# Four segments of attention and feed-forward on one core: the first segment's head in single tiles, and the issue order of all five engines written out as a table

## The chip, the cores and the metric

One core of one Trainium2 chip runs the whole program. The metric is device time in microseconds (us) of one execution, the median of three runs; each compared pair runs on the same chip. A profiled execution of each kernel gives its trace.

## What is computed

The input is 2048 tokens of 640 features in bfloat16. Two rounds of the same two blocks are applied, each added to its input:

```python
x = x + _A_ref(_layernorm(x), wq, wk, wv, wo, beta)   # attention with a memory
x = x + _B_ref(_layernorm(x), w1, w2)                 # relu(x @ w1) @ w2, 640 -> 1728 -> 640
x = x + _A_ref(_layernorm(x), wq, wk, wv, wo, beta)
x = x + _B_ref(_layernorm(x), w1, w2)
```

Block A has 32 heads of 20 features and works through 4 segments of 512 tokens. In each segment it takes causal softmax attention inside the segment, and reads a linear memory `M, z` that the earlier segments have written:

```python
logits = einsum('bhqd,bhkd->bhqk', qs, ks) * scale + mask
a_dot  = softmax(logits) @ vs
a_mem  = (phi(qs) @ M) / (phi(qs) @ z + 1e-6)
outs  += [g * a_mem + (1 - g) * a_dot]
M, z   = M + phi(ks)^T vs, z + sum(phi(ks))
```

## The kernel before

The tokens stand as 16 tiles of 128 (`x_sb`), four to a segment. For each segment the kernel normalizes four tiles (`lnorm`, or `first_pair` for the very first segment), turns them so that features lie on partitions (`xnT`), projects to queries, keys and values, and copies the results from the eight PSUM banks to SBUF. Queries and keys (`stg`) are written to a scratch tensor in DRAM (`spill`, tiles `scr`) and read back by head into `pad` (`fill`), where four heads of 20 rows each lie in four strips of 32 partitions. A fill is four DMAs, one for each strip.

TensorE (PE) then works on pairs of head groups: 8 score halves after each other (`scores`, tiles `ps<-pad`, line L1114), which ScalarE turns into probabilities (`exps`, L1166, tile `PT`) and GpSimd masks (`causal`, L1178); and the value pass (`apply`, L1257, `ps<-PT,v_aug`). Scores use the PE array in four strips of rows, value passes in four strips of columns, everything else uses the whole array. VectorE copies value results out (`av`, L1265), a DMA turns them (`avt`), and `divide` and `combine` make `o_sb`. Then follow the output projection, layer norm and feed-forward (L651 and L654 are the lines of all matmul groups, L1405 the last feature chunk). The memory is read at L1007 (`mem_read`) and written at L1058 (`mem_write`). Where the planner foresees that PE would wait, `keep_busy` puts matmuls of an identity matrix on it (L638, `ps<-ident`), whose results nobody reads; 43 of them warm it at the start (L634).

Everything is written as about 45 streams, generators that yield one operation at a time. The planner `Sched.run` holds a model of the time of each engine and, again and again, takes the operation that can start first, with a priority for each stream. Each engine gets a fixed list, with semaphore waits between engines, so an instruction that waits holds up everything behind it on its engine. SyncE (SP) issues nearly all DMAs, in its own fixed order. The planner runs with 48 values of one cost; `late` replays each plan with DMAs that land late at random, and the plan with the least time is built:

```python
STARTS = [SWITCH_NS + 0.75 * (k - 48 // 2) for k in range(48)]                 # L161
plans = [plan(k, sb, sem_, ...) for k in STARTS]
S = min(plans, key=lambda p: sum(p.late(n) for n in range(4)))
S.P.emit(block)
```

In the head, tiles 0 and 1 of the first segment are one stream (`first_ln_a`: both halves of the statistics at L662, the aggregate at L664, `lnU` at L672, the power on GpSimd at L676, then the normalization `xn_tok` at L716), tiles 2 and 3 another (`first_ln_b`: tile 2's mean and variance by two passes on ScalarE, L764 and L768, tile 3's statistics on VectorE). PE turns each tile with five small matmuls (L739), VectorE or ScalarE copies the result to `xnT` (L745, L746), and `proj_first` projects two tiles at a time, 256 columns wide.

Of the kernel before, what the change touches and what calls it, by code (L numbers as in the profile page):

```python
# [6 lines left out]
dt = mybir.dt  # L7
ACT = mybir.ActivationFunctionType
ALU = mybir.AluOpType
# [164 lines left out]
HOLD_TOL = {"pe": 220.0, "act": 150.0, "dve": 200.0, "pool": 0.0, "sp": 0.0}  # L174


class Sched:


    def __init__(self, prog, switch):  # L180
        self.P = prog
        self.switch = switch
        self.log = []
        self.free = {e: 800.0 for e in ENGS}
        self.t = {}
        self.events = {}
        self.streams = []
        self.dma_free = 0.0
        self.pe_mode = "full"
        self.spare = []  # L190
        self.idle_fn = None

    def keep_busy(self, op, start):

        gap = start - self.free["pe"]
        if gap < IDLE_NS or self.idle_fn is None:
            return
        own = self._pick(op.acq) if op.acq is not None else None
        s = self._pick([x for x in self.spare if x is not own])
        if s is None:  # L200
            return
        begin = max([self.free["pe"]] + [self.at(t) + SEM_NS for t in s.tks])
        n = int((start - begin - IDLE_NS / 2) // (56.0 if begin > COLD_NS else 107.0))
        if n > 1:
            self.log.append(("pe", 56.0 * n, 0.0, s.tks, [], False))
            self.P.waits("pe", s.tks)
            for _ in range(n):
                self.P.op("pe", lambda e, ap=s.ap: self.idle_fn(e, ap), False)

    def add(self, prio, gen):  # L210
        self.streams.append([prio, gen, None, None, False])
# [59 lines left out]
    def run(self):  # L271
        while True:
# [76 lines left out]
            else:  # L349
# [5 lines left out]
                        marks.append(tk)  # L355
                out = marks[0] if len(marks) == 1 else (marks or None)
            self.log.append((e, hold, tail, waits, out if isinstance(out, list) else [out], op.dma is not None))
            st[2], st[3] = None, ((slot, out) if slot is not None else out,)

    def late(self, seed):  # L360

# [26 lines left out]
def pe(ns, fns, waits=(), acq=None, take=(), mode="full"):  # L388
    return Op([("pe", ns, fns, 190.0)], waits, acq=acq, take=take, mode=mode)
# [29 lines left out]
def plan(switch, sb, sem_, psum, dram, A_x, A_wq, A_wk, A_wv, A_wo, A_beta, B_x, B_w1, B_w2, out):  # L419
# [248 lines left out]
    def chain(t0, n, tk, sq=None):  # L668

        sl = slice(t0, t0 + n)  # L670
        if sq is None:
            tk = yield dve(n, 1, lambda e: e.tensor_scalar(lnU[:, sl], mv[:, sl, 1], LN_EPS, None, ALU.add), tk)  # L672
# [3 lines left out]
        tk = yield pool(760, lambda e: e.tensor_tensor(rstd[:, sl], lnU[:, sl], mhalf[:, 0:n], ALU.pow), [tk] + h)  # L676
        return tk

    def turn(slot_sem, dst, src, waits, lat=2000.0):
# [35 lines left out]
    def normed(t, k, bx, tch):  # L715
        return dve(D, 4, lambda e: e.tensor_scalar(  # L716
            bx.ap[:, k * D:k * D + D], x_sb[:, t, :], mv[:, t, 0:1], rstd[:, t:t + 1],
            ALU.subtract, ALU.mult), [tch] + bx.tks, extra=120)

    def first_pair(p, tch):  # L720
        idt = yield Need("ident")
        if p == 0:
            xt = yield Acq(XNT_A)
            xt.users = []
            S.set("xts", 0, 0, tks=[xt])
        else:
            xt = yield Need("xts", 0, 0)
            xt = xt[0]
        bx = yield Acq(XN)
        done = []  # L730
        tns = []
        for k in range(2):
            tn = yield normed(2 * p + k, k, bx, tch[k])
            tns.append(tn)
        for k in range(2):
            t = 2 * p + k
            tn = tns[k]
            pb = lambda bk: bk.ap.bitcast(dt.bfloat16)
            fns = [(lambda e, bk, c=c, k=k: e.transpose(  # L739
                pb(bk)[:, c * 128:(c + 1) * 128], bx.ap[:, k * D + c * 128:k * D + c * 128 + 128], ident[:]),  # L740
                c == FC - 1) for c in range(FC)]
            bk, tT = yield pe((88.0 if p == 0 else 56.0) * FC, fns, [tn] + idt, acq=MISC)
            dst = xt.ap[:, t * FC:(t + 1) * FC, :].rearrange("p c n -> p (c n)")
            src = pb(bk)[:, 0:D]
            tc = yield evac(D, 1.5, lambda e, dst=dst, src=src: e.tensor_copy(dst, src),  # L745
                            lambda e, dst=dst, src=src: e.activation(dst, src, ACT.Copy), [tT])  # L746
            bk.release(tc)
            done.append(tc)
        bx.release(tT)
        S.set("xt", 0, 0, p, tks=done)  # L750

    def first_ln_a():
        tch = []
        for t in range(2):
            w = yield Need(("x0a", "x0b")[t])
            tk = yield from stats(t, w)
            tk = yield from chain(t, 1, [tk])
            tch.append(tk)
        yield from first_pair(0, tch)

    def first_ln_b():
        w = yield Need("x01")
        junk = hT[:, 10:13, :].rearrange("p c n -> p (c n)")[:, 0:D]
        t0 = yield act(D + 350, lambda e: e.activation(  # L764
            junk, x_sb[:, 2, :], ACT.Copy, accum_out=asum[:, 0:1]), w, psum=False)
        tm = yield dve(2, 1, lambda e: e.tensor_scalar(
            mv[:, 2, 0:1], asum[:, 0:1], 1.0 / D, None, ALU.mult), [t0])
        t1 = yield act(D + 470, lambda e: e.activation(  # L768
            junk, x_sb[:, 2, :], ACT.Square, scale=-1.0, bias=mv[:, 2, 0:1],
            accum_out=asum[:, 2:3]), [tm], psum=False)  # L770
        t3 = yield from stats(3, w)
        t1 = yield dve(1, 1, lambda e: e.tensor_scalar(
            lnU[:, 2:3], asum[:, 2:3], 1.0 / D, LN_EPS, ALU.mult, ALU.add), [t1])
        t3 = yield dve(1, 1, lambda e: e.tensor_scalar(lnU[:, 3:4], mv[:, 3, 1:2], LN_EPS, None, ALU.add), [t3])
        h = yield Need("mhalf")
        tch = yield pool(760, lambda e: e.tensor_tensor(
            rstd[:, 2:4], lnU[:, 2:4], mhalf[:, 0:2], ALU.pow), [t1, t3] + h)
        yield from first_pair(1, [tch, tch])


    def proj_ln(a, s):
# [27 lines left out]
    def proj_part(a, s, c, n, h):  # L809
# [767 lines left out]
```

## Time and profile before

| | |
|---|---|
| time, median of 3 runs | 562.49 us (562.12 to 563.04) |
| the profiled execution's own time | 562.46 us |
| its span in the trace | 560.6 us, so 1.86 us lie outside |
| instructions in the trace | 12651 |
| busy share: PE, VectorE (DVE), ScalarE (ACT), GpSimd (POOL) | 99%, 73%, 73%, 35% |

The page gives the busy time of each engine, the span in 40 slices, the DMA queues, the chain of work that ended last, and the costliest groups of instructions. In the timeline a row is: start in us, duration in us, engine, line, operation, output tile `<-` input tiles, shapes, and how many equal instructions it merges; a bracket tells the idle time before it and what ended it. A matmul's duration in a row includes its way through the array, so rows of PE overlap; the spacing between the starts of two rows tells how long the first one held the array.

### The profile page before, as it was taken

The numbers are of one execution on the slowest core, as the hardware profiler recorded it, in microseconds if no ns is written. First come the engines' busy times: TensorE is split into PE (matmuls) and PEld (weight loads), VectorE is DVE, ScalarE is ACT, GpSimd is POOL, SyncE is SP. The second block draws the span as 40 slices with busy tenths as digits, with TensorE's granted clock in tenths as the row PEclk, the third lists the DMA queues.
The fourth block names the chain that finished last, engine by engine and source line by source line (L and its number), as shares of the span: only waits on it lengthen the run. The fifth ranks groups of instructions, "written<-read, shape, count | busy, mean of one in ns | idle before, by whom it ended". The sixth has DMA issues, their size and how long they took to land.

```text
span 560.6 us, 12651 instructions
## 1 busy us (share of the span) xinstructions
PE 555.5 (99%) x5110; PEld 302.6 (54%) x5111; DVE 410.8 (73%) x1060; ACT 409.7 (73%) x522; POOL 194.3 (35%) x302
## 2 busy tenths in 40 slices
PE   8999999999999999999999999999999999999998
PEld 7654545545644455645356554465445654665655
DVE  5898899776998787877888987889824866651202
ACT  5799999987699779787897789877856788323140
POOL 4534344333354444344433443335401433100000
DMA  8599988741374137443373505550325510422101
GB/s 269 118 201 219 254 202 164 172 123 44 90 175 99 50 89 185 88 99 79 97 179 52 127 20 137 131 120 20 67 77 154 114 43 20 93 69 55 41 1 47
DMA packets 132219, 61.43 MB, mean 110 GB/s; under 512 B 111042, under 2 KB 122050, under 8 KB 132162
## 3 DMA queue, kind: packets, MB, share of 16 engines
q1 hardware_dynamic: 131942, 60.37, 45.7%
q8 instruction: 40, 0.66, 0.5%
q10 hardware_dynamic: 220, 0.26, 0.2%
q14 instruction: 17, 0.14, 0.1%
HBM read 20.57 MB, written 12.85 MB: 60 GB/s over the span
## 4 chain that ended last, share of the span: by engine, by line
PE 90%; DVE 8%; DMA 1%; ACT 0%; POOL 0%; issue 0%
PE ps L654 58%; PE ps L651 12%; PE ps L1114 9%; PE ps L1257 7%; DVE stats L662 2%; PE ps L1058 2%; PE ps L1007 2%; DVE x_sb L1328 1%; PE ps L1405 1%; DVE stg L827 1%; DMA x_sb<-in_A_x_dram 1%; DVE xn_tok L704 1%; DVE av L1265 0%; DVE xn_tok L716 0%; DVE mv L664 0%; ACT PT L1166 0%
## 5 line engine op out<-in xcount | busy, mean ns | idle before, releaser
L1166 ACT ACTIVATE PT<-ps 128x1024 bf16<-128x1024 f32 x320 | 310.1, 1022 | 66.1 <-PE ps L1114 64.5
L1178 POOL TENSOR_SCALAR_AFFINE_SELECT PT<-PT 128x512 bf16<-128x512 bf16 x256 | 166.3, 668 | 267.7 <-ACT PT L1166 267.7
L654 PE MATMUL ps<-w_r,hT 128*128 128x320 bf16 (+2 forms) x768 | 123.4, 299 | 0.1
L654 PE MATMUL ps<-xnT,w_r 128*128 128x512 bf16 x416 | 113.6, 379 | 0.0
L1328 DVE TENSOR_TENSOR x_sb<-x_sb,ps 128x320 bf16<-128x320 bf16 (+1 forms) x128 | 60.4, 479 | 70.2 <-PE ps L654 69.9
L654 PEld LDWEIGHTS ps<-w_r,hT 128*128 128x128 bf16 x768 | 72.2, 98 | 34.2 <-issue 6.3
L1436 ACT ACTIVATE hT<-ps 128x512 bf16<-128x512 f32 x55 | 33.0, 599 | 46.4 <-PE ps L654 46.1
L1114 PE MATMUL ps<-pad 20*128 20x384 bf16 (+3 forms) x1024 | 64.9, 301 | 0.0
L654 PEld LDWEIGHTS ps<-xnT,w_r 128*128 128x128 bf16 x416 | 39.7, 98 | 42.1 <-issue 2.9
L662 DVE BATCH_NORM_STATS2 stats<-x_sb 128x6 f32<-128x320 bf16 x126 | 55.9, 470 | 2.3 <-DMA x_sb<-in_A_x_dram 2.0
L1265 DVE CAST av<-ps 128x512 bf16<-128x512 f32 x56 | 38.3, 684 | 12.9 <-PE ps L1257 12.5
L1114 PEld LDWEIGHTS ps<-pad 20*128 20x128 bf16 x1024 | 18.2, 92 | 51.4 <-ACT PT L1166 24.2
L654 PE MATMUL ps<-wo_r,oT 128*128 128x320 bf16 x256 | 45.3, 299 | 0.0
L1434 DVE TENSOR_SCALAR hT<-ps 128x512 bf16<-128x512 f32 x49 | 33.5, 684 | 10.5 <-PE ps L654 10.0
L1257 PE MATMUL ps<-PT,v_aug 128*32 128x256 bf16 (+5 forms) x896 | 40.7, 302 | 0.0
L651 PE MATMUL ps<-xnT,w_r 128*128 128x512 bf16 x104 | 39.6, 381 | 0.0
L654 PE MATMUL ps<-wv_r,xnT 128*128 128x320 bf16 x192 | 35.8, 300 | 0.0
L654 PE MATMUL ps<-xnT,wk_r 128*128 128x512 bf16 (+1 forms) x140 | 35.5, 349 | 0.0
L676 POOL TENSOR_TENSOR rstd<-lnU,mhalf 128x2 f32<-128x2 f32 (+2 forms) x25 | 20.3, 811 | 39.9 <-DVE lnU L672 39.7
L654 PE MATMUL ps<-xnT,wq_r 128*128 128x512 bf16 (+1 forms) x140 | 33.9, 349 | 0.0
L1301 DVE TENSOR_TENSOR o_sb<-avt,rden 128x320 bf16<-128x320 bf16 x60 | 33.3, 572 | 0.7
L654 PEld LDWEIGHTS ps<-wo_r,oT 128*128 128x128 bf16 x256 | 24.8, 98 | 11.3 <-issue 1.3
(120 smaller groups left out, 686.9 us busy)
## 6 DMA issues: line engine op xcount, KB each, us to landing
pad<-scr SPq DMA_DIRECT2D x124, 80.0 KB
scr<-stg SPq DMA_DIRECT2D x34, 256.0 KB, 2.9
out_dram<-x_sb SPq DMA_DIRECT2D x15, 160.0 KB, 1.8
w_r<-in_B_w_dram SPq DMA_DIRECT2D x10, 216.0 KB, 3.3
w_r<-in_B_w_dram SPq DMA_DIRECT2D x13, 160.0 KB, 2.7
x_sb<-in_A_x_dram SPq DMA_DIRECT2D x9, 160.0 KB, 3.3
scr<-w_r SPq DMA_DIRECT2D x5, 256.0 KB, 3.5
x_sb<-in_A_x_dram SPq DMA_DIRECT2D x3, 320.0 KB, 7.3
```

The source lines that it names most:

```text
L651: bk, tk = yield pe(mm_ns(n), [(lambda e, bk, a=a, b=b: e.matmul(bk.ap[:, 0:n] if len(b.shape) == 2 else bk.ap[:, 0:n].rearrange("p (i n) ...
L654: tk = yield pe(mm_ns(n), [(lambda e, k=k, a=a, b=b, bk=bk: e.matmul(bk.ap[:, 0:n] if len(b.shape) == 2 else bk.ap[:, 0:n].rearrange("p (i ...
L662: tk = yield dve(320, 1, lambda e, c2=c2: e.bn_stats(stats6[:, t, c2, :], x_sb[:, t, c2 * 320:(c2 + 1) * 320]), xt)
L1114: fns.append([(lambda e, z=z, j=j, hh=hh, N=N, o=o, sl=sl: e.matmul(ps[:, hh, o:o + N], sl.ap[32 * hh:32 * hh + DH, z, 0, 128 * j:128 * j ...
L1166: tx = yield act(1024, lambda e, dst=dst, src=src: e.activation(dst, src, ACT.Exp, scale=SCALE), sc + pw)
L1178: tm = yield pool(600.0, lambda e, reg=reg: e.affine_select(out=reg, in_=reg, pattern=[[0, 4], [1, 128]], compare_op=ALU.is_ge, fill=0.0, ...
L1257: fns.append((lambda e, bk, j=j, hh=hh, pt=pt, g=g0 + z: e.matmul(bk.ap[32 * hh:32 * hh + wide(g, hh), 128 * j:L], VAUG[vx(a, s)][:, j].re ...
L1265: te = yield evac(L, 1, lambda e, sl=sl, z=z, bk=bk: e.tensor_copy(sl.ap[:, z], bk.ap), lambda e, sl=sl, z=z, bk=bk: e.activation(sl.ap[:, ...
L1301: to = yield dve(320, 1, lambda e, dst=dst, src=src, rz=rz: e.tensor_tensor(dst, src, rz, ALU.mult), [tg] + OSB.tks)
L1328: ta = yield dve(n, 1, lambda e: e.tensor_tensor(x_sb[:, t, c0:c0 + n], x_sb[:, t, c0:c0 + n], bk.ap[:, 0:n], ALU.add), [tk] + list(waits) ...
L1434: th = yield evac(512, 1, lambda e, dc=dc, bk=bk: e.tensor_scalar(hT[:, dc, :], bk.ap[:, :], 0.0, None, ALU.max), lambda e, dc=dc, bk=bk: ...
L1436: lambda e, dc=dc, bk=bk: e.activation(hT[:, dc, :], bk.ap[:, :], ACT.Relu), [tk] + HT.tks)
```

## The change

The change has two parts.

**The head goes by single tiles.** `first_ln_a`, `first_ln_b` and `first_pair` are replaced by four streams `first_tile(t)`. Tiles 0 and 1 keep their statistics on VectorE; tiles 2 and 3 both get theirs from ScalarE, two passes each. A list `TURN` tells the planner in which order VectorE takes the steps of tiles 0 to 3, and each tile has its own power on GpSimd. PE projects tile 0 and tile 1 for the first two chunks of keys and queries one tile at a time (`proj_tile`, 128 columns wide) and leaves both in the same PSUM bank; the rest of the first segment is projected as before.

**The order of the streams on every engine is written out.** The planner runs once (`STARTS = [79.0]`) and records each operation with its stream. `in_turns` then rebuilds the program with the order of the streams on each engine taken from the strings in `TURNS`, one letter for each operation; the waits are put in anew, and the operations of one stream keep their order. The strings come from replays in which DMAs and engines are late at random. The dependencies between operations stay as the planner recorded them, and so do the buffers.

```diff
-STARTS = [SWITCH_NS + 0.75 * (k - 48 // 2) for k in range(48)]
+STARTS = [79.0]
...
+TURNS = {
+    "sp": (
+        "HHHHHHHHHGllllmllmyyllllsmIIIIIlmIlslellmIllylmysIelmmIIIIIIlImllllIIlImlllslggymmIIIyllemmlIIskjell"
...
+    def in_turns(self, turns):
+
+        names = "abcdefghijklmnopqrstuvwxyzABCDEFGHIJKLMNOPQRSTUVWXYZ"
+        todo = {e: {} for e in ENGS}
+        for r in self.record:
+            todo[r[0]].setdefault(names[r[1]], []).append(r)
+        seq = {e: [r for r in self.record if r[0] == e] for e in ENGS}
+        for e, order in turns.items():
...
+            its = {n: iter(rs) for n, rs in todo[e].items()}
+            seq[e] = [next(its[n]) for n in order]
+        P = Prog(self.P.clk)
...
-        tk = yield pool(760, lambda e: e.tensor_tensor(rstd[:, sl], lnU[:, sl], mhalf[:, 0:n], ALU.pow), [tk] + h)
+        tk = yield pool(600, lambda e: e.tensor_tensor(rstd[:, sl], lnU[:, sl], mhalf[:, 0:n], ALU.pow), [tk] + h)
...
+    TURN = ["s0", "s0", "a0", "s1", "l0", "s1", "n0", "m2", "a1", "l1", "m3", "c0", "n1", "l2", "c1"]
...
+    def first_tile(t):
+        p, k = divmod(t, 2)
+        w = yield Need(("x0a", "x0b", "x01", "x01")[t])
+        if p == 0:
+            for c2 in range(2):
+                tk = yield from in_turn("s%d" % t, dve(320, 1.1, lambda e, c2=c2: e.bn_stats(
...
+        else:
+            junk = hT[:, 10 - 3 * k:13 - 3 * k, :].rearrange("p c n -> p (c n)")[:, 0:D]
+            ta = yield act(D + 350, lambda e: e.activation(
+                junk, x_sb[:, t, :], ACT.Copy, accum_out=asum[:, t:t + 1]), w, psum=False)
...
+        tch = yield pool(560, lambda e: e.tensor_tensor(
+            rstd[:, t:t + 1], lnU[:, t:t + 1], mhalf[:, 0:1], ALU.pow), [tk] + h)
...
+    def proj_tile(t, n, c):
...
+        for k in range(FC):
+            mm = lambda e, bk, k=k: e.matmul(
+                bk.ap[:, 128 * t:128 * t + 128], w_r[:, k, c * 128:(c + 1) * 128],
+                xt.ap[:, t * FC + k, :], start=(k == 0), stop=(k == FC - 1))
...
     def proj_first():
-        order = [(c, n, h) for h in range(2) for c in range(2) for n in range(2)]
-        order += [(c, n, h) for c in range(2, FC) for h in range(2) for n in range(2)]
+        for t in range(2):
+            for n in range(2):
+                for c in range(2):
+                    yield from proj_tile(t, n, c)
+        order = [(2, 0, 0)] + [(c, n, 1) for c in range(2) for n in range(2)]
...
-    S.add(5, first_ln_a())
-    S.add(5, first_ln_b())
+    for t in range(4):
+        S.add(1 + 0.2 * t, first_tile(t))
...
-            S.P.emit(block)
+            S.in_turns(TURNS).emit(block)
```

Three places show what moves. The lines of the changed kernel have other numbers: L742 is its warm-up, L746 its identity matmuls, L893 the turning of the first tiles, L976 `proj_tile`, L759 and L762 the matmul groups, L1275 the scores, L1418 the value pass, L1168 the memory read, L1106 the fill, L1061 the spill, L790 a turning DMA.

PE at the start, before (wk_r and wq_r are the key and query weights):

```order
L634 MATMUL ps<-ident 128x128 x43
L638 MATMUL ps<-ident 128x128 x10
L739 MATMUL ps<-ident,xn_tok 128x128 x10
L638 MATMUL ps<-ident 128x128 x5
L739 MATMUL ps<-ident,xn_tok 128x128 x10
L651 MATMUL ps<-xnT,wk_r 128x256
L654 MATMUL ps<-xnT,wk_r 128x256 x4
```

PE at the start, now:

```order
L742 MATMUL ps<-ident 128x128 x43
L893 MATMUL ps<-ident,xn_tok 128x128 x5
L746 MATMUL ps<-ident 128x128 x9
L893 MATMUL ps<-ident,xn_tok 128x128 x5
L976 MATMUL ps<-xnT,wk_r 128x128 x10
L976 MATMUL ps<-xnT,wq_r 128x128 x5
L893 MATMUL ps<-ident,xn_tok 128x128 x5
L976 MATMUL ps<-xnT,wq_r 128x128 x5
L976 MATMUL ps<-xnT,wk_r 128x128 x8
L893 MATMUL ps<-ident,xn_tok 128x128 x5
```

The first projection stands behind two turned tiles instead of four, and no identity matmuls stand between the warm-up and the first turning.

VectorE at the same place, before (the first tiles' statistics, `mv` the mean and variance, `lnU` the input of the power):

```order
L662 BN_STATS stats<-x_sb 128x6 x2
L664 BN_AGGR mv<-stats 128x2
L672 TENSOR_SCALAR lnU<-mv 128x1
L662 BN_STATS stats<-x_sb 128x6 x2
L766 TENSOR_SCALAR mv<-asum 128x1
L664 BN_AGGR mv<-stats 128x2
L662 BN_STATS stats<-x_sb 128x6
L672 TENSOR_SCALAR lnU<-mv 128x1
L662 BN_STATS stats<-x_sb 128x6
L716 TENSOR_SCALAR xn_tok<-x_sb,mv,rstd 128x640
```

VectorE, now:

```order
L853 BN_STATS stats<-x_sb 128x6 x3
L855 BN_AGGR mv<-stats 128x2
L853 BN_STATS stats<-x_sb 128x6
L857 TENSOR_SCALAR lnU<-mv 128x1
L863 TENSOR_SCALAR mv<-asum 128x1
L855 BN_AGGR mv<-stats 128x2
L857 TENSOR_SCALAR lnU<-mv 128x1
L863 TENSOR_SCALAR mv<-asum 128x1
L824 TENSOR_SCALAR xn_tok<-x_sb,mv,rstd 128x640 x2
```

Tile 3's two statistics halves are gone from in front of the first normalization; one half of tile 1 and the means of tiles 2 and 3 stand ahead of it.

SP in the first round's third segment, before (the third row is the fill of the 12th pair of head groups):

```order
L682 DMA_TRANSPOSE avt<-av 128x8x128
L682 DMA_TRANSPOSE oT<-o_sb 128x10x128 x2
L945 DMA pad<-scr 20x2x1024 x4
L682 DMA_TRANSPOSE avt<-av 128x8x128
L682 DMA_TRANSPOSE xnT<-xn_tok 128x10x128
L900 DMA scr<-stg 128x1024 x3
L682 DMA_TRANSPOSE xnT<-xn_tok 128x10x128
L682 DMA_TRANSPOSE avt<-av 128x8x128
L945 DMA pad<-scr 20x2x1024 x4
```

SP at the same pair, now:

```order
L790 DMA_TRANSPOSE oT<-o_sb 128x10x128 x2
L790 DMA_TRANSPOSE avt<-av 128x8x128
L1106 DMA pad<-scr 20x2x1024 x7
L1061 DMA scr<-stg 128x1024 x3
L790 DMA_TRANSPOSE xnT<-xn_tok 128x10x128 x2
L790 DMA_TRANSPOSE avt<-av 128x8x128
L1106 DMA pad<-scr 20x2x1024 x3
```

The seven fill DMAs are the whole 11th pair and three strips of the 12th; its fourth strip is now the first of the later three, behind three spills and three turning DMAs. Over the whole program 2 of 31 fills were broken up by other DMAs before, and 23 are now, 18 of them by turning DMAs.

Counted over the whole order of PE: 5111 matmuls before and 5138 now (54 identity matmuls of `keep_busy` before and 61 now, of which 39 and 52 stand behind the first projection; 20 projections of 256 columns are now 40 of 128); uninterrupted runs of scores 164 before and 166 now; stretches on the whole array between them 174 and 169; 60 value passes and 8 last chunks of the feed-forward in both.

More of the change, by code (lines that the diff above doesn't have):

```diff
@@ L206, in keep_busy @@
             self.P.waits("pe", s.tks)
-            for _ in range(n):
-                self.P.op("pe", lambda e, ap=s.ap: self.idle_fn(e, ap), False)
+            fns = [(lambda e, ap=s.ap: self.idle_fn(e, ap), False)] * n
+            for fn, mark in fns:
+                self.P.op("pe", fn, mark)
+            self.record.append(("pe", len(self.streams), fns, None, s.tks, [], s, "full", 56.0 * n))
     def add(self, prio, gen):
@@ L718, in normed, with my_turn, in_turn @@
             ALU.subtract, ALU.mult), [tch] + bx.tks, extra=120)
-    def first_pair(p, tch):
+    HALF = {0: [], 1: []}
+    TURN = ["s0", "s0", "a0", "s1", "l0", "s1", "n0", "m2", "a1", "l1", "m3", "c0", "n1", "l2", "c1"]
+    def my_turn(what):
+        k = CALLED.get(what, 0)
+        CALLED[what] = k + 1
+        i = [j for j, w in enumerate(TURN) if w == what][k]
+        if i:
+            yield Need("turn", i - 1)
+        return i
+    CALLED = {}
+    def in_turn(what, op):
+        i = yield from my_turn(what)
+        r = yield op
+        S.set("turn", i, tks=[])
+        return r
@@ L725, in first_pair @@
             S.set("xts", 0, 0, tks=[xt])
-        else:
[L727 to L778, printed above, removed]
@@ new lines, in first_tile @@
+        if k == 0:
+            bx = yield Acq(XN)
+            S.set("bx", p, tks=[bx])
+        xt = yield Need("xts", 0, 0)
+        bx = yield Need("bx", p)
+        xt, bx = xt[0], bx[0]
+        if p == 0:
+            tn = yield from in_turn("n%d" % t, normed(t, k, bx, tch))
+        else:
+            tn = yield normed(t, k, bx, tch)
+        pb = lambda bk: bk.ap[:, 0, :].bitcast(dt.bfloat16)
+        fns = [(lambda e, bk, c=c: e.transpose(
+            pb(bk)[:, c * 128:(c + 1) * 128], bx.ap[:, k * D + c * 128:k * D + c * 128 + 128], ident[:]),
+            c == FC - 1) for c in range(FC)]
@@ new lines, in first_tile @@
+        bk, tT = yield pe((88.0 if t == 0 else 56.0) * FC, fns, [tn] + idt, acq=[X, Y])
+        dst = xt.ap[:, t * FC:(t + 1) * FC, :].rearrange("p c n -> p (c n)")
+        src = pb(bk)[:, 0:D]
+        if p == 0:
+            tc = yield from in_turn("c%d" % t, dve(D, 1.5, lambda e: e.tensor_copy(dst, src), [tT], urgent=True))
+        else:
+            tc = yield evac(D, 1.5, lambda e: e.tensor_copy(dst, src),
+                            lambda e: e.activation(dst, src, ACT.Copy), [tT])
+        bk.release(tc)
@@ L781, in proj_ln @@
+        HALF[p].append((t, tT, tc))
+        S.set("xtt", t, tks=[tc])
+        if len(HALF[p]) == 2:
+            bx.release(*[x[1] for x in HALF[p]])
+            S.set("xt", 0, 0, p, tks=[x[2] for x in sorted(HALF[p])])
     def proj_ln(a, s):
```

128 lines of the change are left out of this document (127 added, 1 removed).

## The prediction

> **What bounds the kernel now.** I read the page first, then PE's timeline around the few places where it waits, last the timeline of the head.
>
> ```profile
> PE 555.5 (99%) x5110; PEld 302.6 (54%) x5111; DVE 410.8 (73%) x1060; ACT 409.7 (73%) x522; POOL 194.3 (35%) x302
> PE 90%; DVE 8%; DMA 1%; ACT 0%; POOL 0%; issue 0%
> ```
>
> The first row is the page's busy time, the second the chain that ended last, by engine. PE is busy for 99% of the span and carries 90% of the chain; the other engines have a quarter of their time free. So the time is the sum of what stands on PE, plus the few places where PE waits. The order of the others matters only where it makes PE wait.
>
> Matmul ends are modelled, so the spacing of starts tells where PE waits. PE's timeline at five places:
>
> ```profile
> 58.33 0.57 PE L654 MATMUL ps<-wv_r,hT 128*128 128x320 bf16 x3
> 58.86 0.98 PE L1058 MATMUL ps<-v_aug,phk 128*128 128x147 bf16 x12
> ...
> 79.47 0.62 PE L638 MATMUL ps<-ident 128*128 128x128 bf16 x8
> 80.36 0.34 PE L1007 MATMUL ps<-BD,w_r 128*128 128x84 bf16 x3 [0.27 <-DVE om_sb L1018]
> ...
> 97.23 0.33 PE L1007 MATMUL ps<-BD,w_r 128*128 128x147 bf16 x3
> 97.41 0.30 PE L654 MATMUL ps<-wv_r,xnT 128*128 128x320 bf16 x1
> ...
> 99.87 0.34 PE L1007 MATMUL ps<-BD,w_r 128*128 128x147 bf16 x3
> 100.47 0.31 PE L651 MATMUL ps<-wv_r,xnT 128*128 128x320 bf16 x1 [0.25 <-DVE av L1265]
> ...
> 324.17 0.38 PE L654 MATMUL ps<-xnT,w_r 128*128 128x512 bf16 x1
> 324.64 0.29 PE L638 MATMUL ps<-ident 128*128 128x128 bf16 x2
> ```
>
> Three memory-read matmuls hold PE 0.18 us at 97.23 and 0.60 us at 99.87: 0.42 lost. Eight identity matmuls of 128 columns, at half of what 256 columns take in the head (0.109, below), need 0.44 us, and the next row comes after 0.89: 0.45 lost. The row at 324.17 holds PE 0.47 us where 512 columns need 0.21 (below): 0.26 lost. Three matmuls of 320 columns need 0.41 and have 0.53 at 58.33: 0.12 lost; I find five gaps of about this size behind the head, which I put at 0.5 together. All waits there come to 1.6 us, which is all that a better order can win.
>
> **What one piece costs on PE.**
>
> ```profile
> 321.81 0.38 PE L651 MATMUL ps<-xnT,wk_r 128*128 128x512 bf16 x1
> 322.02 0.38 PE L654 MATMUL ps<-xnT,wk_r 128*128 128x512 bf16 x1
> 322.34 0.39 PE L1114 MATMUL ps<-pad 20*128 20x512 bf16 x4
> 322.66 0.39 PE L654 MATMUL ps<-xnT,wk_r 128*128 128x512 bf16 x1
> ...
> 324.86 0.40 PE L1114 MATMUL ps<-pad 20*128 20x384 bf16 x8
> 325.19 0.73 PE L1257 MATMUL ps<-PT,v_aug 128*32 128x512 bf16 x16
> ```
>
> A matmul of 512 columns holds PE 0.21 us before another of its kind and 0.32 before scores: leaving the whole array costs 0.10. The scores hold it 0.32 until the next row. A run of eight holds it no longer (0.33 at 324.86), so each run into which a round is split costs another 0.32.
>
> - Score runs, 164 to 166: 2 x 0.32 = +0.65.
> - Stretches on the whole array, 174 to 169: 5 x 0.10 = -0.5.
> - Identity matmuls behind the first projection, 39 to 52: 13 x 0.055 = +0.7. They are fixed work: where a wait that they fill doesn't come, they cost all the same.
> - All other matmuls behind the head are the same in number and size.
>
> **The head.**
>
> ```profile
> 1.59 4.77 PE L634 MATMUL ps<-ident 128*128 128x128 bf16 x43 [1.59 <-POOL mhalf L587]
> 3.79 0.89 DVE L662 BATCH_NORM_STATS2 stats<-x_sb 128x6 f32<-128x320 bf16 x2 [1.96 <-DMA x_sb<-in_A_x_dram]
> 4.63 2.12 SPq L511 DMA_DIRECT2D wv_r<-in_A_wv_dram  x1
> 4.86 0.74 ACT L764 ACTIVATE hT<-x_sb 128x640 bf16<-128x640 bf16 x1 [2.11 <-DMA x_sb<-in_A_x_dram]
> 5.19 0.56 POOL L676 TENSOR_TENSOR rstd<-lnU,mhalf 128x1 f32<-128x1 f32 x1 [3.61 <-DVE lnU L672]
> 5.50 0.19 ACT L764 ACTIVATION_READ_ACCUMULATOR hT<-x_sb 128x1 f32 x1
> 6.15 1.05 PE L638 MATMUL ps<-ident 128*128 128x128 bf16 x10
> 6.87 0.43 DVE L716 TENSOR_SCALAR xn_tok<-x_sb,mv,rstd 128x640 bf16<-128x640 bf16 x1
> 7.36 0.45 PE L739 MATMUL ps<-ident,xn_tok 128*128 128x128 bf16 x5 [0.15 <-DVE xn_tok L716]
> 7.88 0.48 DVE L745 COPY xnT<-ps 128x640 bf16<-128x640 bf16 x1
> 9.06 0.81 PE L739 MATMUL ps<-ident,xn_tok 128*128 128x128 bf16 x10 [0.19 <-DVE xn_tok L716]
> 9.71 0.27 PE L651 MATMUL ps<-xnT,wk_r 128*128 128x256 bf16 x1
> 10.25 0.27 PE L651 MATMUL ps<-xnT,wq_r 128*128 128x256 bf16 x1
> 14.07 0.30 PE L651 MATMUL ps<-wv_r,xnT 128*128 128x320 bf16 x1
> wv_r<-in_A_wv_dram SPq DMA_DIRECT2D x1, 800.0 KB, 8.8
> ```
>
> The last row is the DMA view's (KB, us from issue to landing): the value weights, issued at 4.63, land at 13.43.
>
> Before, tile 0's power ends at 5.75 and its normalization starts only at 6.87, behind tile 3's statistics. Now one more statistics half (0.45) stands ahead of the power, which then ends near 6.3, and VectorE waits for tile 3's mean: two ScalarE passes of 0.83 from 4.86 end at 6.5, the small step at 6.65. Normalization to 7.1, turning at 7.15 (0.2 earlier). The copy follows in the same 0.52 and takes 0.48: ready at 8.15. On PE five turnings (0.3), nine identity matmuls (0.5) and tile 1's five (0.3) reach to 8.3. So the first projection starts at 8.3 instead of 9.71.
>
> That isn't 1.4 us won, since two tiles are still to be turned: 10 small matmuls at 0.065 (9.06 to 9.71) are 0.65, and 40 projections of 128 columns at 0.055 take 2.2 where 20 of 256 took 2.2 (five in 0.545, 9.71 to 10.25). The first value matmul stands behind these and 17 projections of 256 columns (1.85): 8.3 + 0.65 + 2.2 + 1.85 = 13.0. The weights land at 13.43, so PE waits there and goes on at about 13.5. The kernel before had done the same 37 projections at 9.71 + 37 x 0.109 = 13.75. What is won is 0.25 to 0.3 us; 0.7 if the weights came 0.4 us earlier, and nothing if the first turning came 0.7 us later, since the wait takes up the first 0.45. The new wait holds up PE's projections behind it, for which nobody waits yet.
>
> **The new waits.** A table of turns can't take over the old waits one for one. Nothing in the trace of before shows them; the bounds are zero and, from the only row-by-row measure of how well a fixed list meets this chip, about the old 1.6. I take half, 0.8, since the places that waited (memory reads behind VectorE at 80 and 100 us) are rearranged, but the fills now land closer to their use (below). Cover that may go: ScalarE and VectorE have a quarter of their time free, so a late probability or eviction costs PE only where scores stand directly behind it.
>
> Sum against the profiled execution: 562.46 - 0.3 + 0.65 - 0.5 + 0.7 - 1.6 + 0.8 = 562.2. The median of the runs is 562.49, so the same holds for it. The tail, feed-forward matmuls alone, is the same list.
>
> **Rivals.**
>
> *Fills come late (slower).* A score run waits for all four DMAs of its fill.
>
> ```profile
> 142.40 1.66 SPq L945 DMA_DIRECT2D pad<-scr  x4
> ...
> 157.91 2.35 SPq L900 DMA_DIRECT2D scr<-stg  x3
> ...
> 162.56 1.31 SPq L682 DMA_TRANSPOSE avt<-av  x1
> 163.98 1.59 SPq L945 DMA_DIRECT2D pad<-scr  x4
> ...
> 170.46 0.40 PE L1114 MATMUL ps<-pad 20*128 20x512 bf16 x4
> xnT<-xn_tok SPq DMA_TRANSPOSE x26, 3.6
> ```
>
> Before, the 12th pair's fill is issued at 142.40, 28 us ahead of its first scores at 170.46. Now its fourth DMA stands behind the spills and turning DMAs that SP issues from 157.91 on, each of which waits for VectorE; the next DMA behind them went out at 163.98. With a landing like that of the nearest row, 3.6, it is there at 167.6, some 1 to 3 us ahead of the scores. Eighteen fills are split so. It decides where SP comes two us later than in these rows. If a third of the 18 cost PE 0.4 us each beyond what I have taken, that is 6 x 0.4 = 2.4: 564.6. Against it: most have more room, and PE's place moves little. 0.20.
>
> *The waits vanish (faster).* The weights land in time (-0.75 instead of -0.3) and the new waits come to 0.2: 562.46 - 0.75 + 0.65 - 0.5 + 0.7 - 1.6 + 0.2 = 561.2. For it: all the waits of before are small near-ties. Against it: the landing is set by the same queue of loads. 0.13.
>
> *PE is still slow when the head starts.* The 43 warm-up matmuls come 0.11 us apart, the later ones 0.055 to 0.065; the change of pace falls into the ten identity matmuls at 6.15, which are now gone, with PE idle from 6.2 to 7.15. [...] 0.12. [...]
>
> **How the numbers follow.** Forecast 0.55, fills 0.20, no waits 0.13, pace 0.12. Runs of this kernel differ by some 0.1%, so 0.2% (1.1 us) is about what a measurement can tell from no change. The likeliest time is 562.2, its own range, with new waits of 0.1 to 1.6, 561.5 to 563.0. With the other cases I take 561.1 to 564.0, which leaves out the upper half of the late fills. Within 0.2% lie the forecast and the slow pace, 0.67; faster is the case without waits, 0.13; slower the late fills, 0.20.
>
> **What would show it.** The first projection at about 8.3 us and a wait for a DMA ahead of the first value matmul near 13.4; PE busy 99% again; fewer than 1 us of PE gaps behind the head, none over 0.5. The forecast is wrong if PE's waits name `pad` or a turned tile as releaser for more than 1 us in all (fills), or if the first small projections come 0.11 us apart (pace). Should the head win a full us at the first value matmul, my reading of the weights' landing is wrong.

## The result: 565.13 us, slower by half a per cent

| | before | after |
|---|---|---|
| median of 6 runs each, us | 562.47 (562.06 to 563.04) | 565.13 (564.09 to 566.95) |
| the profiled execution, us | 562.46 | 565.24 |
| span, us | 560.6 | 563.2 |

The ratio is 1.0051 (95% interval 1.0035 to 1.0066). The forecast was 562.2 with a range of 561.1 to 564.0, so the time lies outside, on the slower side.

The page of the changed kernel: busy time by engine, and the chain that ended last.

```profile
PE 555.1 (99%) x5138; PEld 303.3 (54%) x5138; DVE 410.8 (73%) x1065; ACT 407.4 (72%) x519; POOL 195.7 (35%) x303
PE 89%; DVE 7%; DMA 2%; ACT 1%; issue 0%; POOL 0%; SPq 0%; ACTq 0%; DVEq 0%
```

By the page nothing has happened: PE is as busy as before, within 0.4 us, and the span is 2.6 us longer. (Another 0.2 us lie outside the span: 2.04 to 2.12 us of each of the six executions, where each execution of the kernel before on record has 1.81 to 1.93.) What is longer is a place where PE stands. PE's waits by what ended them (us in total, times, longest), changed kernel:

```profile
PE ps L759 <- ACT stg L959: 2.6, 1, 2.6
PE ps L742 <- POOL mhalf L695: 1.6, 1, 1.6
PE ps L893 <- DVE xn_tok L824: 1.2, 1, 1.2
PE ps L759 <- DVE w_r L958: 0.2, 1, 0.2
PE ps L759 <- DMA oT<-o_sb: 0.2, 1, 0.2
```

One wait of 2.6 us is new: a value matmul (L759) waits for ScalarE's copies of keys and queries out of PSUM (`stg`, L959). The next two rows are the start, the first turning included. No row names `pad`. The timeline around the new wait, changed kernel (SPq and ACTq are DMA issues from SyncE and ScalarE; L721 is the exponential of beta for the gate, L1135 that of phi):

```profile
7.51 0.45 PE L893 MATMUL ps<-ident,xn_tok 128*128 128x128 bf16 x5 [1.16 <-DVE xn_tok L824]
8.16 0.93 SPq L718 DMA_DIRECT2D beta_bc<-in_A_beta_dram  x1
8.58 0.72 PE L976 MATMUL ps<-xnT,wk_r 128*128 128x128 bf16 x10
...
13.08 0.63 ACT L1135 ACTIVATE phs<-stg 128x512 bf16<-128x512 bf16 x1
13.35 0.30 PE L759 MATMUL ps<-wv_r,xnT 128*128 128x320 bf16 x1
14.91 0.71 PE L762 MATMUL ps<-wv_r,xnT 128*128 128x320 bf16 x4
16.25 0.23 ACT L721 ACTIVATE gt<-beta_bc 128x32 f32<-128x32 bf16 x1 [2.53 <-DMA beta_bc<-in_A_beta_dram]
16.25 1.44 ACTq L1085 DMA_DIRECT2D pad<-stg  x1
17.74 0.66 ACT L959 ACTIVATE stg<-ps 128x256 bf16<-128x256 f32 x2 [1.27 <-DVE stats L770]
18.18 0.31 PE L759 MATMUL ps<-wv_r,xnT 128*128 128x320 bf16 x1 [2.57 <-ACT stg L959]
```

ScalarE is done with the first phi exponential at 13.71. The next in its list is the exponential of beta, and it waits 2.53 us for the load of beta. Behind it stands a DMA that ScalarE issues itself, 1.44 us, and only then come the two copies that would free PSUM banks. The four value matmuls of the row at 14.91 end their hold on PE at 15.45; for the next there is no bank, and PE stands until 18.18, 2.73 us. (Here and below, a hole is the spacing of two starts less what such a pair takes elsewhere.) The bracket at 17.74 names a VectorE instruction as the one that ended the idle time; the row above it, ScalarE's own issue, fills just this stretch.

The DMA view shows how late beta lands. First the rows of the changed kernel (KB, us from issue to landing), then beta's row and the timeline of the kernel before:

```profile
wv_r<-in_A_wv_dram SPq DMA_DIRECT2D x1, 800.0 KB, 8.1
beta_bc<-in_A_beta_dram SPq DMA_DIRECT2D x1, 8.0 KB, 8.1
```

```profile
beta_bc<-in_A_beta_dram SPq DMA_DIRECT2D x1, 8.0 KB, 2.6
17.52 0.49 SPq L610 DMA_DIRECT2D beta_bc<-in_A_beta_dram  x1
21.99 0.24 ACT L613 ACTIVATE gt<-beta_bc 128x32 f32<-128x32 bf16 x1
```

Before, beta was issued at 17.52, after the big loads, took 2.6 us, and its exponential ran at 21.99 without a wait. In the written table it is SP's tenth DMA, issued at 8.16 directly behind all weights and tokens of the head, and takes 8.1 us for 8 KB (in the profiled executions of three other kernels below that have it at this place 6.6 in the first and the third experiment and about 6.7 in the fourth, so the landing shown here is the slowest of them). Beta lands at 16.26, behind the value weights, which were issued ahead of it and land at 13.2. VectorE needs the result only at 28.84, as the timeline of the changed kernel goes on:

```profile
28.84 0.17 DVE L722 TENSOR_SCALAR gt<-gt 128x32 f32<-128x32 f32 x1
```

### The profile page after: what moved, and what is told of

Read it like the earlier page. It is cut to its first block, busy times and chain, and to the rows that moved or that the text cites. A ratio compares the mean times of both kernels' runs of the same rounds, so it can differ in the third digit from the quotient of the medians.

```text
span 563.2 us, 12714 instructions
## 1 busy us (share of the span) xinstructions
PE 555.1 (99%) x5138; PEld 303.3 (54%) x5138; DVE 410.8 (73%) x1065; ACT 407.4 (72%) x519; POOL 195.7 (35%) x303
## 4 chain that ended last, share of the span: by engine, by line
PE 89%; DVE 7%; DMA 2%; ACT 1%; issue 0%; POOL 0%; SPq 0%; ACTq 0%; DVEq 0%
PE ps L762 57%; PE ps L759 11%; PE ps L1275 9%; PE ps L1418 6%; PE ps L1168 2%; PE ps L1219 1%; DVE stats L770 1%; DMA oT<-o_sb 1%; DVE w_r L958 1%; DVE xn_tok L812 1%; PE ps L1566 1%; DMA x_sb<-in_A_x_dram 1%; PE ps L746 1%; DVE av L1426 1%; PE ps L1369 1%; DVE o_sb L1462 1%
## 5 line engine op out<-in xcount | busy, mean ns | idle before, releaser
L762 PE MATMUL ps<-w_r,hT 128*128 128x320 bf16 (+2 forms) x768 | 124.2, 299 | 0.0
L762 PE MATMUL ps<-xnT,w_r 128*128 128x512 bf16 x416 | 112.7, 379 | 0.0
L762 PEld LDWEIGHTS ps<-w_r,hT 128*128 128x128 bf16 x768 | 72.0, 98 | 33.5 <-issue 6.1
L1275 PE MATMUL ps<-pad 20*128 20x512 bf16 (+3 forms) x1024 | 65.7, 301 | 0.0
L762 PEld LDWEIGHTS ps<-xnT,w_r 128*128 128x128 bf16 x416 | 38.9, 98 | 41.8 <-issue 3.5
L1597 ACT ACTIVATE hT<-ps 128x512 bf16<-128x512 f32 x59 | 35.4, 599 | 30.6 <-PE ps L762 30.1
L770 DVE BATCH_NORM_STATS2 stats<-x_sb 128x6 f32<-128x320 bf16 x120 | 53.1, 472 | 0.1
L1426 DVE CAST av<-ps 128x512 bf16<-128x512 f32 x54 | 37.0, 685 | 15.6 <-PE ps L1418 15.1
L762 PE MATMUL ps<-wo_r,oT 128*128 128x320 bf16 x256 | 47.2, 299 | 0.0
L1275 PEld LDWEIGHTS ps<-pad 20*128 20x128 bf16 x1024 | 18.4, 92 | 49.5 <-ACT PT L1327 23.7
L1418 PE MATMUL ps<-PT,v_aug 128*32 128x256 bf16 (+5 forms) x896 | 40.7, 302 | 0.0
L784 POOL TENSOR_TENSOR rstd<-lnU,mhalf 128x2 f32<-128x2 f32 (+1 forms) x23 | 19.4, 843 | 58.7 <-DVE lnU L780 53.2
L759 PE MATMUL ps<-xnT,w_r 128*128 128x512 bf16 x104 | 39.6, 381 | 0.0
L762 PE MATMUL ps<-wv_r,xnT 128*128 128x320 bf16 x192 | 36.5, 299 | 0.0
L1595 DVE TENSOR_SCALAR hT<-ps 128x512 bf16<-128x512 f32 x45 | 30.2, 679 | 7.0 <-PE ps L762 6.4
L762 PE MATMUL ps<-xnT,wk_r 128*128 128x512 bf16 (+1 forms) x132 | 34.5, 353 | 0.0
L958 DVE CAST stg<-ps 128x512 bf16<-128x512 f32 (+1 forms) x44 | 27.4, 632 | 8.9 <-PE ps L762 8.7
L762 PE MATMUL ps<-xnT,wq_r 128*128 128x512 bf16 (+1 forms) x132 | 33.0, 354 | 0.0
L1462 DVE TENSOR_TENSOR o_sb<-avt,rden 128x320 bf16<-128x320 bf16 x60 | 31.7, 547 | 0.3
```

The source lines that it names most:

```text
L759: bk, tk = yield pe(mm_ns(n), [(lambda e, bk, a=a, b=b: e.matmul(bk.ap[:, 0:n] if len(b.shape) == 2 else bk.ap[:, 0:n].rearrange("p (i n) ...
L762: tk = yield pe(mm_ns(n), [(lambda e, k=k, a=a, b=b, bk=bk: e.matmul(bk.ap[:, 0:n] if len(b.shape) == 2 else bk.ap[:, 0:n].rearrange("p (i ...
L770: tk = yield dve(320, 1, lambda e, c2=c2: e.bn_stats(stats6[:, t, c2, :], x_sb[:, t, c2 * 320:(c2 + 1) * 320]), xt)
L958: te = yield evac(N, 1, lambda e, sg=sg, bk=bk: e.tensor_copy(sg.ap[:, t0:t0 + N], bk.ap[:, 0:N]), lambda e, sg=sg, bk=bk: e.activation(sg ...
L1275: fns.append([(lambda e, z=z, j=j, hh=hh, N=N, o=o, sl=sl: e.matmul(ps[:, hh, o:o + N], sl.ap[32 * hh:32 * hh + DH, z, 0, 128 * j:128 * j ...
L1418: fns.append((lambda e, bk, j=j, hh=hh, pt=pt, g=g0 + z: e.matmul(bk.ap[32 * hh:32 * hh + wide(g, hh), 128 * j:L], VAUG[vx(a, s)][:, j].re ...
```

## The experiments

Theory A was the wait just read: ScalarE's wait for beta, and what it holds up, is the whole loss. Theory B put the loss into the rest of the written table or into the head. Each kernel was timed against the kernel before on the same chip; its medians were 562.57 to 562.78 there.

**The gate's exponential later on ScalarE.** In ScalarE's string of turns one letter moves 14 places back; the load of beta stays where it is.

```diff
-        "HwxwxwzzzzzGoGlzzCzColClCzbbzobbbbbbzoCbb...
+        "HwxwxwzzzzzGolzzCzColClCzbbGzobbbbbbzoCbb...
```

> The changed kernel with one instruction moved: ScalarE's exponential of beta (gt<-beta_bc) goes from behind the first exponential of phi to behind the first pair of softmax exponentials, some 8 us later; nothing else moves. Theory A (ScalarE stands 2.5 us at this instruction for the beta load, and PE loses 2.6 us behind it at the value projections): PE's gap at 15 us is gone, 562.3 to 562.8, ratio to before 1.000 +- 0.001. Theory B (the loss belongs to the written order as a whole and only shows first at this place): the gap comes back at a later place, over 564.

Measured: 562.75 us, ratio 0.9998 (0.9988 to 1.0007). That is 2.4 us less than the changed kernel and the same as the kernel before. Timeline of this kernel:

```profile
8.53 0.47 SPq L718 DMA_DIRECT2D beta_bc<-in_A_beta_dram  x1
13.20 1.34 ACTq L1085 DMA_DIRECT2D pad<-stg  x1
13.25 0.30 PE L759 MATMUL ps<-wv_r,xnT 128*128 128x320 bf16 x1 [0.32 <-ACT phs L1135]
14.59 0.66 ACT L959 ACTIVATE stg<-ps 128x256 bf16<-128x256 f32 x2 [1.34 <-PE ps L762]
15.35 0.30 PE L759 MATMUL ps<-wv_r,xnT 128*128 128x320 bf16 x1
```

ScalarE's issue follows at once, the copies run at 14.59 instead of 17.74, and the value matmul at 15.35 does not wait. So without the wait the whole loss against the kernel before is gone. What is left is a hole of 0.49 us ahead of the first value matmul at 13.25; the bracket gives 0.32 of it to ScalarE, but the value weights, issued at 4.60 with 8.5 us to landing, are there only at 13.1.

**The load of beta early.** The other cure: beta is SP's third DMA, and ScalarE's order stays as changed.

```diff
-        "HHHHHHHHHGllll...
+        "HHGHHHHHHHllll...
```

> The changed kernel with one DMA moved: SP issues the load of beta as its third DMA instead of its tenth, ahead of the weights; ScalarE's order is as in the changed kernel. Theory A: the load lands by 5 us, ScalarE does not stand at the exponential of beta, 562.3 to 562.9 (the weights are issued 0.4 us later, which the wait at the first value matmul may show as up to 0.4). Theory B: over 564. If the load is still slow because of its 32-byte rows and not because of its place behind the weights, the wait stays in part.

Measured: 563.65 us, ratio 1.0015 (1.0004 to 1.0026), between the two theories. Beta, issued at 1.71, took 4.9 us and so landed at 6.6 instead of the expected 5, but still long before its use. (Its rows are 64 bytes, 8 KB over 128 partitions, and not 32.) PE's waits of this kernel:

```profile
PE ps L759 <- DMA wv_r<-in_A_wv_dram: 1.0, 1, 1.0
PE ps L976 <- DMA wk_r<-in_A_wk_dram: 0.4, 1, 0.4
PE ps L976 <- DMA wq_r<-in_A_wq_dram: 0.3, 1, 0.3
```

The wait for ScalarE is gone here too, which confirms the cause by a second way, but each weight behind beta is later (the first key weights land at 10.0 instead of 8.4, the value weights at 14.7 instead of 13.2), and PE waits for three of them. This cure costs about 0.9 us against the first one, 563.65 against 562.75.

**The old kernel with the new place of the gate.** The program of the kernel before, with beta as SP's tenth DMA and its exponential directly behind ScalarE's first phi exponential; nothing else moves.

```diff
+GATE_AT = 12
...
+        seq["sp"].insert(9, beta)
...
+        seq["act"].insert(GATE_AT, gate)
```

> The kernel before with the suspected wait put in: its own order on every engine, but the load of beta directly behind SP's tenth place (after the loads, as in the changed kernel) and the exponential of beta directly behind ScalarE's first exponential of phi. Theory A: ScalarE stands about 2.5 us until the load lands near 16.2, evictions behind it are late, PE loses 1.5 to 2.6 us near 15 to 18 us: 564.0 to 565.2. Theory B: the wait is taken up by free PSUM banks, under 563.

Measured: 563.22 us, ratio 1.0012 (1.0002 to 1.0021), less than expected. Its timeline:

```profile
14.88 0.23 ACT L653 ACTIVATE gt<-beta_bc 128x32 f32<-128x32 bf16 x1 [1.15 <-DMA beta_bc<-in_A_beta_dram]
15.02 0.64 ACT L868 ACTIVATE stg<-ps 128x256 bf16<-128x256 f32 x2
15.44 0.31 PE L691 MATMUL ps<-wv_r,xnT 128*128 128x320 bf16 x1
```

The load lands earlier here (6.6 us), ScalarE waits 1.15, and the copies stand directly behind the exponential, without a DMA to issue in between. PE loses 0.31 us. So the place alone isn't the price. Two things are smaller here, the wait, since beta landed at 14.88 instead of 16.25, and what stands between it and the copies that PE needs; this run doesn't separate them.

**ScalarE's issue behind the copies.** The changed kernel as it is, with its wait for beta; only the DMA issue (`l`) goes behind the two copies (`zz`).

```diff
-        "HwxwxwzzzzzGoGlzzCzC...
+        "HwxwxwzzzzzGoGzzlCzC...
```

> The changed kernel as it is, with ScalarE still waiting for beta behind the first phi exponential; only the DMA that ScalarE issues behind the gate (pad<-stg) now stands behind the two evictions of stg instead of ahead of them. Theory A, PE stands for all that lies ahead of those evictions on ScalarE, the wait of 2.53 and the issue of 1.44 us: the evictions end about 1.3 us earlier, PE's gap falls from 2.73 to about 1.4 and the time from 565.1 to 563.8. Theory B, the landing of beta alone sets the gap and an issue costs ScalarE nothing: the gap stays at 2.7, 565.1.

Measured: 564.43 us, ratio 1.0032 (1.0020 to 1.0044): 0.7 less than the changed kernel, about half of what A expected. The two intervals overlap (1.0020 to 1.0044 here, 1.0035 to 1.0066 for the changed kernel), so the times alone don't decide against B's nothing; the timeline does.

```profile
13.74 0.30 PE L759 MATMUL ps<-wv_r,xnT 128*128 128x320 bf16 x1 [0.85 <-DMA wv_r<-in_A_wv_dram]
15.53 0.23 ACT L721 ACTIVATE gt<-beta_bc 128x32 f32<-128x32 bf16 x1 [2.33 <-DMA beta_bc<-in_A_beta_dram]
15.67 0.64 ACT L959 ACTIVATE stg<-ps 128x256 bf16<-128x256 f32 x2
16.09 0.31 PE L759 MATMUL ps<-wv_r,xnT 128*128 128x320 bf16 x1
17.79 0.28 PE L759 MATMUL ps<-xnT,wk_r 128*128 128x256 bf16 x1 [0.30 <-ACT w_r L1040]
```

The copies now start 0.14 us after the exponential's start instead of 1.49, so here ScalarE no longer stands for its issue ahead of them. PE's hole at this place shrinks from 2.73 to 0.26, but the issue now delays the next copies, and PE has two more holes, 0.46 at 17.19 and 0.24 at 18.02. In this execution beta also landed 0.7 earlier and the value weights 0.4 later than in the changed kernel's, so the split between wait and issue is only roughly known.

**The head alone.** The changed kernel with the planner's order instead of the written turns, first with its one plan, then with the best of 48 plans, as in the kernel before.

```diff
-            S.in_turns(TURNS).emit(block)
+            S.P.emit(block)
```

> The changed kernel without the written turns: the single plan at 79.0 is built as the planner orders it, with the head by single tiles. Theory A: the exponential of beta stands where the planner puts it; if the planner also puts it ahead of the landing, the loss of 2.6 us is that of the head and not of the turns (565), otherwise 562 to 564 by the planner's own near-ties. Theory B (written turns cost through late fills and split rounds): 562 or less, fills unbroken.

> The changed kernel's head by single tiles, but the planner's own order instead of the written turns, and the plan with the least replayed time out of 48 as in the kernel before (with one plan it took 564.97). Theory A, the head itself is worth its 0.3 us and the planner's choice among 48 is as good as before: 562.2. Theory B, the new head shifts all streams so that the near-ties fall worse whatever the plan: 564 or more, as with one plan.

Measured: 564.97 (ratio 1.0034, 1.0022 to 1.0046) and 564.87 (1.0045, 1.0032 to 1.0058). With one plan neither theory came true: beta plays no part, since SP issues it only behind six other DMAs that take it from 14.74 to 19.46, and yet the time is that of the changed kernel. With 48 plans theory B's 564 or more came. The second plan's waits on PE behind the head:

```profile
PE ps L1168 <- DVE w_r L1136: 0.6, 1, 0.6
PE ps L759 <- DVE av L1426: 0.3, 1, 0.3
PE ps L1168 <- DVE om_sb L1179: 0.3, 1, 0.3
PE ps L1168 <- DVE BD L1240: 0.3, 1, 0.3
```

PE's holes behind 10 us, counting those of 0.1 us and more, come to 2.7 with the second plan, where the kernel before has 1.35 by the same measure; 13 more identity matmuls are 0.7 and two more score runs 0.65. So the planner's order around the new head loses 2.2 to 2.3 us, and the written turns, with the gate moved, win about as much back (562.75 against 564.97 with one plan, on the same chip). The written turns with the old head were not tried, since the table fits this program alone.

**Without identity matmuls behind the head.** All 52 left out; the gate stays moved back, as in the first experiment.

> The changed kernel with the gate's exponential moved back (562.75 in the first runs), without the 52 identity matmuls behind the first projection; they have no result that anything reads. Theory A, they are fixed work standing where waits no longer come: 52 x 0.055 = 2.9 us less, 559.9, and the gaps of PE behind the head stay at 1.5 us. Theory B, each fills a wait that comes anyway: the gaps grow by 2.9 us and the time stays at 562.75. The prediction's term for them, 13 more of them for 0.7, holds only under A.

Measured: 565.04 us, ratio 1.0045 (1.0033 to 1.0056): 2.3 us more than with them. Below is a table by stage of this kernel (each engine's busy time, then PE's granted clock, DMA share and GB/s), and PE's timeline in its third stage:

```profile
core 0: us, PE busy (x) PEld busy (x) DVE busy (x) ACT busy (x) POOL busy (x), PEclk, DMA share, GB/s
76.00:79.00 3.00, 2.98 (x51) 1.45 (x47) 2.97 (x12) 2.73 (x4) 1.57 (x3) 1.00 0.48 76
79.00:83.00 4.00, 2.47 (x32) 0.95 (x33) 3.97 (x10) 4.00 (x6) 3.44 (x6) 0.92 0.97 210
83.00:89.40 6.40, 6.40 (x34) 2.69 (x35) 3.81 (x11) 3.81 (x5) 1.86 (x3) 0.52 0.93 236
...
81.01 0.39 PE L1277 MATMUL ps<-pad 20*128 20x384 bf16 x4 [0.53 <-ACT PT L1329]
82.95 0.50 PE L1170 MATMUL ps<-BD,w_r 128*128 128x84 bf16 x3 [0.57 <-DVE om_sb L1181]
85.94 1.01 PE L764 MATMUL ps<-wo_r,oT 128*128 128x320 bf16 x3
86.74 0.47 PE L761 MATMUL ps<-wo_r,oT 128*128 128x320 bf16 x1
```

Both theories fall short. PE's holes grow by some 5.4 us (the small ones of the slow stretch counted too), against 2.9 saved. Waits in the places of identity matmuls do come, about 2 us of holes between 78.5 and 82.9, and then PE's clock drops to half (1.00 granted until 79.0, 0.92 until 83.0, 0.52 until 89.4): three matmuls of 320 columns hold PE for 0.80 us (85.94 to 86.74) where they need 0.41. By this spacing the slow stretch costs about 2.6 us itself. The waits cost even without it: one of the six executions kept the full clock and took 564.05. What brings the clock down isn't shown; in this timeline no two rows ahead of the slow stretch start more than 0.96 us apart (81.99 to 82.95).

**The first value matmul later.** In the head of the first experiment, the lone value matmul goes behind 13 projections, where the weights have surely landed.

```diff
-        "FuJJvz...zzzzCzzzzzzzzzzzzzCCCCCCCCCCCCC...
+        "FuJJvz...zzzzzzzzzzzzzzzzzCCCCCCCCCCCCCC...
```

> The changed kernel with the gate's exponential moved back, and the first value matmul behind the last query projections instead of inside a key projection, 13 matmuls of 256 columns (1.4 us) later. Theory A, PE's gap of 0.49 us at 12.65 is the landing of the value weights alone, and the weights are there 1.4 us later: the gap goes, 562.3. Theory B, the rest of the head (evictions, banks) is as late as the weights: the gap comes back a few matmuls later and the time stays at 562.75.

Measured: 562.66 us, ratio 0.9998 (0.9990 to 1.0007), no gain. PE's hole of 0.49 is gone, as A said; in its place PE waits twice for probabilities around 71 and 74 us:

```profile
PE ps L1275 <- ACT PT L1327: 0.5, 2, 0.3
```

Windows of the kernel of the first experiment suggest why (columns as above):

```profile
60.00:80.00 20.00, 20.00 (x258) 10.94 (x256) 18.75 (x54) 19.15 (x26) 8.30 (x13) 1.00 0.69 188
400.00:500.00 100.00, 100.00 (x892) 55.20 (x885) 66.27 (x162) 62.28 (x77) 29.74 (x45) 1.00 0.35 81
```

Between 60 and 80 us VectorE is busy for 18.75 and ScalarE for 19.15 of 20 us. So what PE wins ahead of this stage it can lose again there, as it did in this profiled execution; that this holds for every execution isn't shown. The room that the page's 72% promise lies mostly behind 400 us. A kernel with this edit and without the 52 identity matmuls behaved like that without them, and its expected 559.4 is refuted:

> The changed kernel with the gate's exponential moved back, without the 52 identity matmuls behind the first projection, and with the first value matmul behind the last query projections. If both theories A hold: 562.75 - 2.9 - 0.45 = 559.4, below the kernel before by 0.6%. If the identity matmuls fill waits that come anyway: 562.3. If neither holds: 562.75.

Measured: 565.02 us, ratio 1.0046 (1.0032 to 1.0060).

**The last holes mended.** With the gate moved back, PE's string is edited behind 200 us, and the 8 identity matmuls at 429 and 451 us are left out. The first kernel has three places, the second only the first two.

```diff
-iiiiiadAD ... rDDDD ... CCCCCAAaC
+ADiiiiiad ... DDDDr ... AACCCCaCC
```

> The changed kernel with the gate's exponential moved back (562.75), and PE's turns mended at the three places behind 200 us where it still stood: two projections ahead of the output projection that waited for the turned tile oT (0.72), four feed-forward matmuls ahead of a memory read (0.22), two key projections ahead of five value matmuls (0.15); and without the 8 identity matmuls at 429 and 451 us, where without them PE stood no longer (0.44). Theory A, these are the last waits and nothing takes their place, since the other engines have room behind 200 us: 0.43 + 0.22 + 0.15 + 0.44 = 1.2 less, 561.5, below the kernel before by 0.2%. Theory B, a gain on PE meets another engine a little later as in the first 100 us: 562.5 or more.

Measured: 562.91 us, ratio 1.0012 (1.0000 to 1.0023). The profiled execution, 564.48, shows three misses, of which two stand here (PE's waits, then ScalarE's timeline):

```profile
PE ps L1277 <- ACT PT L1329: 1.2, 2, 1.1
PE ps L761 <- DVE av L1428: 0.5, 1, 0.5
70.32 0.63 ACT L1137 ACTIVATE w_r<-w_r 128x512 bf16<-128x512 bf16 x1 [1.79 <-DVE rtmp L1130]
```

The second row is of my making: the key projections put ahead need a bank that VectorE hasn't freed, 0.64 us of hole in place of 0.15. The first is not, since nothing is edited before 200 us: in this execution ScalarE waited 1.79 us for VectorE ahead of the probabilities, where the same instruction waited 0.32 in the first experiment's execution. The third is an output projection that now waits 0.7 us for its turned tile at 372 us.

> The changed kernel with the gate's exponential moved back (562.75), two projections ahead of the output projection that waited for oT (0.43), four feed-forward matmuls ahead of a memory read (0.22), and without the 8 identity matmuls at 429 and 451 us (0.44). Unlike the kernel with three mended places, the five value matmuls near 333 us stay where they were: moving them back had turned a wait of 0.15 into one of 0.64. Theory A, at these places nothing else is late: 562.75 - 1.1 = 561.7, below the kernel before. Theory B, what a fixed order loses from execution to execution in the first 100 us hides so small a gain: 562.3 to 562.8.

Measured with two places: 561.95 us (561.54 to 563.86), the kernel before 562.78 (562.33 to 563.09), ratio 0.9994 (0.9985 to 1.0003). The median is 0.8 us lower, but the interval holds no change, so it isn't shown to beat the kernel before.

## Why the prediction was wrong

- **The failed step is "the new waits", 0.8.** PE's holes behind 10 us, counting those of 0.1 us and more, are 3.8 us, against 1.35 before by the same measure; 2.73 is the one hole at 15.45, and 0.94 are the other three behind it. So for all places but one the term was about right, and with that one it measured 3.7, outside its bounds of 0.1 to 1.6. The statement that stood behind it, "ScalarE and VectorE have a quarter of their time free, so a late probability or eviction costs PE only where scores stand directly behind it", is wrong twice. A late eviction also holds up any matmul that needs its bank, and this is what cost the 2.73. And the room is an average that the stretch from 20 to 100 us doesn't have: there each of the two engines is busy for some 18 to 19 us of every 20 (windows of the first experiment's kernel). The sum never asked what else the table had moved on ScalarE and SP in the head, where beta's load and its exponential both went ahead.
- **The rest of the sum holds.** With that wait taken out (first experiment) the profiled execution took 562.9 where 562.2 was forecast, and its holes are 1.5 behind the head where 0.8 was taken. With the holes and the head as measured, two score runs more, five leavings fewer and 13 identity matmuls more fit the measured span to about 0.3 us. A term that the sum had at nothing is the time outside the span: every execution of a kernel with the new head has 2.01 to 2.13 us there, with the written table or without it, and every one of the kernel before 1.81 to 1.93. That is 0.2 us, and the traces don't show what it is.
- **The head** came as worked out: first projection at 8.58 (8.3 forecast), first value matmul at 13.35 (13.5), the value weights landed at 13.2. By the prediction's own count the kernel before is as far at 13.75, so the head wins 0.4 us there (0.5 in the first experiment, at 13.25) instead of 0.3, and 0.2 of it goes outside the span.
- **Identity matmuls** were priced as fixed work that costs "all the same". For the 8 behind 400 us that holds: without them no hole came. For most of the others the wait comes, and without them the clock fell too, in 10 of 12 executions of the two kernels (mean granted 0.994 to 0.997).
- **The rivals.** *Fills come late* gave nearly the right time, 564.6, for the wrong reason: no wait on PE names `pad`. *The waits vanish* is refuted by the holes. *PE is still slow* is refuted by ten projections in 0.56 us from 8.58 on; how long a slow pace would have lasted there, and what it would have cost, no run shows. The test named in the text, no hole over 0.5 us behind the head, is what failed.
- What stays open: why the planner's own order around the new head meets more near-ties with each of the two plans built, and what the 0.2 us outside the span are.

## What to carry to other kernels

Where an order is written out, look first at the instructions that wait for a DMA and stand on an engine's list ahead of what frees a buffer for the bottleneck: the price here was the wait (2.53 us) and a DMA issue (1.44) between it and that release, although the waiting instruction's own result was needed 12 us later. Here a load of 8 KB queued behind large ones landed only behind them, at 16.26 us where the 800 KB of the value weights landed at 13.2, so its consumer has to be placed by the landing and not by its size. And an engine with time to spare on the page may have none in the stage that matters (73% and 72% on the page here, some 18 to 19 of every 20 us between 20 and 100 us): read the busy time by stage before a delay is called free.

## What was not expected of the hardware

- 8 KB took 8.1 us from issue to landing as the last of the head's loads, 6.6 in two other kernels at the same place and about 6.7 in a third, 4.9 as the third load, and 2.6 when issued at 17.52.
- A DMA issued by ScalarE held its next instruction up by 1.3 to 1.4 us in the head (the copies start at 14.59 behind an issue at 13.20).
- PE's clock fell to half (0.52 granted for 6.4 us) after 4 us in which PE was busy for 2.47, with no two rows that start more than 0.96 us apart. One hole of 2.73 us in the changed kernel's profiled execution did not do that: the matmuls behind it at 18.33 run at the full pace (four of 320 columns in 0.54 us, granted clock 1.00). Two of that kernel's six executions, 566.95 and 565.87, do have a mean clock of 0.997; they have no trace that shows where.
